# Weight conversion of a fused attention and mixer kernel: a compare-and-multiply on VectorE becomes a maximum on GpSimd

## The chip, the cores and the metric

The kernel runs on one core of one Trainium2 chip. The metric is device time in microseconds (us) of one execution, as the median of several runs. The engines are TensorE (PE in the rows, its weight loads PEld), VectorE (DVE), ScalarE (ACT), GpSimd (POOL) and SyncE (SP, which issues most DMAs). Each engine works through its own queue in order.

## The reference, cut to what matters

Three stages follow one another: attention inside clusters, a channel mixer with a gate, and a token and channel mixer. All inputs are float32. The weights of the two mixers reach the kernel as 64-bit words.

```
xr = mu_r*x + (1-mu_r)*x_prev ; xk = mu_k*x + (1-mu_k)*x_prev
k  = relu(xk @ w_k) ; v = (k*k) @ w_v ; x = sigmoid(xr @ w_r) * v
h  = relu(x^T @ w_tok1) @ w_tok2 ; u = x + h^T
out = u + relu(u @ w_ch1) @ w_ch2
```

Shapes: batch 2, sequence 768, model width 512, w_k 512x1024, w_v 1024x512, w_r 512x512, w_tok1 768x256, w_tok2 256x768, w_ch1 512x1536, w_ch2 1536x512.

## The kernel before, in words

The attention stage (up to about 200 us) is laid out by a planner and is the same in both kernels. The mixers are matrix products in which each operand is split into a high and a low part, and three products (high by high, high by low, low by high) are added in PSUM.

Weights come in units of 128 x 512 values: wr 0 to 3 (gate), wk and wv 0 to 7 (first mixer), w1 and w2 0 to 2 (token mixing), c1 and c2 0 to 11 (channel mixing), 52 conversions in all with wk 0 and wv 0 loaded a second time. A DMA brings a unit as 64-bit words into a ring of five buffers (`wraw`), seen as two interleaved 32-bit halves, `low` and `high`. `w_split` turns it into a float32 value in `g` and then into the two parts of `wu`. In the kernel before the steps are: a shift and mask of `high` (VectorE, L460), the sign bits joined in (VectorE, L464), the absolute value of `high` (ScalarE, L468, into the second half of `wu`), the bits of `low` joined in (VectorE, L470, after which the ring buffer is free and the next DMA is issued), a compare with `TINY` times the value (VectorE, L478), the rounded copy (ScalarE, L482) and the rest (VectorE, L484; GpSimd for the four wr units). The compare makes a weight zero whose `high` half, read as a float32, lies under `TINY`: the shift would have given it a wrong exponent.

`g` has two buffers, and at most two conversions are under way at once. From the end of the attention stage on (`dense[0]` is true) a list scheduler in the program, `pump`, writes out the order of the instructions: every conversion, evacuation and operand split is a `Chain`, a generator that names for each step its engine, a cost in us and whether it is a step with two SBUF inputs ("two"). `now` holds a modelled clock for each engine; `lock` keeps the modelled GpSimd steps ("G") and the two-input VectorE steps apart. The scheduler takes, of the steps that can start first, the one of the chain with the earliest due time. What it decides fixes the queue of each engine.

The first mixer runs over f = 0 to 7 for batch 0 and back for batch 1: 24 matmuls of wk f (L1354) make the hidden part f, ScalarE and VectorE square and split it (L1323 to L1329, `hl`), and 18 matmuls with wv f (L1392) add to the output, one f behind. While batch 0 runs, VectorE and ScalarE also prepare the mixed operand of batch 1 (`mk1`: L555, L557, L564, L566, four parts). The token mixer follows (L1448, L1534), then the channel mixer.

Of the kernel before, what the change touches and what calls it, by code (L numbers as in the profile page):

```python
# [13 lines left out]
AF = mybir.ActivationFunctionType  # L14
ALU = mybir.AluOpType
# [3 lines left out]
P = 128  # L19
B, H, S, D = 2, 8, 768, 64  # L20
# [19 lines left out]
TINY = 2.0**-15 * 1.125  # L40
# [258 lines left out]
def f32(ap):  # L299
    return ap.bitcast(F32)  # L300
# [3 lines left out]
def cluster_attention_moe_mixer(ctx: ExitStack, tc, q, k, v, cent, mu_k, mu_r, w_k, w_v, w_r, w1, w2, wc1, wc2, out):  # L304
    nc = tc.nc
# [38 lines left out]
            nc.gpsimd.memset(t[:, :, 0:1], 0.0)  # L344


    now = {"P": 0.0, "A": 0.0, "D": 0.0, "G": 0.0, "S": 0.0, "N": 0.0, "R": 0.0}
    lock = [0.0, 0.0]
    pipe = []

# [59 lines left out]
    dense = [False]  # L410
# [29 lines left out]
    def w_issue():  # L440
        key = seq.pop(0)
        ring.append(ring.pop(0))
        raw = ring[-1][0].tile([P, 1024], U32, tag=ring[-1][1], name="wraw")
        src = unit_src(*key)
        dst = raw.rearrange("p (k f) -> p k f", f=src.shape[-1]) if len(src.shape) == 3 else raw
        nc.sync.dma_start(out=dst, in_=src)
        now["S"] = max(now["S"], now["D"])
        staged.append((key, max(now["S"], now["D"]) + RAW_US, raw.rearrange("p (f w) -> p f w", w=2)))

    def w_split():  # L450
        key, landed, raw = staged.pop(0)
        low, high = raw[:, :, 0], raw[:, :, 1]
        pool, tag, freed = free_slots.pop(0)
        t = pool.tile([P, 2, 512], F32R, tag=tag, name="wu")

        def gen():
            yield "D", 0.45, False
            g = cvt.tile([P, 512], U32, tag="g", name="g")
            gf = f32(g)
            nc.vector.tensor_scalar(  # L460
                g, high, 3, 0x3FFFFFF8, op0=ALU.logical_shift_left, op1=ALU.bitwise_and
            )
            yield "D", 0.62, True
            nc.vector.scalar_tensor_tensor(  # L464
                out=g, in0=high, scalar=0xC0000000, in1=g, op0=ALU.bitwise_and, op1=ALU.bitwise_or
            )
            yield "A", 0.56, False
            nc.scalar.activation(t[:, 1, :], f32(high), AF.Abs)  # L468
            yield "D", 0.62, True
            nc.vector.scalar_tensor_tensor(  # L470
                out=g, in0=low, scalar=29, in1=g, op0=ALU.logical_shift_right, op1=ALU.bitwise_or
            )
            if wanted:
                spare.append((ring.pop(0), wanted.clear())[0])
            elif dense[0] and seq:
                w_issue()
            yield "D", 0.62, True
            nc.vector.scalar_tensor_tensor(  # L478
                out=gf, in0=f32(t[:, 1, :]), scalar=TINY, in1=gf, op0=ALU.is_ge, op1=ALU.mult
            )  # L480
            yield "A", 0.55, False
            nc.scalar.activation(t[:, 0, :], gf, AF.Copy)  # L482
            yield ("G", 1.4, True) if key[0] == "wr" else ("D", 0.62, True)
            (nc.gpsimd if key[0] == "wr" else nc.vector).tensor_tensor(  # L484
                out=t[:, 1, :], in0=gf, in1=f32(t[:, 0, :]), op=ALU.subtract
            )
            if key in again_from:
                yield "S", 0.55, False
                nc.sync.dma_start(out=again_from[key], in_=f32(t).rearrange("p a f -> p (a f)"))

        ch = Chain(gen(), due.get(key, 0.0), max(landed, freed))
        active[:] = [c for c in active if not c.done] + [ch]
        units[key] = (t, ch)
        slot_of[key] = (pool, tag)
        return ch
# [18 lines left out]
    def feed():  # L514
        while staged and free_slots and staged[0][0] not in units and sum(not c.done for c in active) < 2:
            w_split()
        while reloads and free_slots and not staged and not seq:
            w_reload()
        for wait in list(later):
            if wait[0]():  # L520
                later.remove(wait)
                wait[1]()
# [3 lines left out]
    def need(key):  # L526
        while key not in units:
            if not dense[0]:
                if not staged:
                    w_issue()  # L530
                w_split()
            else:
                pump(None)
        t, ch = units[key]
        after(ch)
        return t
# [82 lines left out]
    with ExitStack() as actx:  # L619
# [453 lines left out]
        def want(n, key, j=0.0):  # L1073
            return T_FIRST + PER * (n + (EARLY.get(n, LATE.get(n - NP, {})).get(key, DUE[key]) + j) / NTASK)
# [62 lines left out]
        for n in range(NP):  # L1137
# [22 lines left out]
            if n + 1 < NP:  # L1160
# [13 lines left out]
                t = o = simt_[n] = Op("P", 0.66, want(n, "simt"), act("simt"), [o], tail=0.2, need=1)  # L1174
# [37 lines left out]
        for i in range(NEARLY + 2):  # L1212
            t = want(NP - 5, f"wr{i}", NTASK * i) if i < KD else want(NP - 1, "wl", i - KD)
            landed.append(Op("S", 0.5, t - 60 if i < KD else t - 10, w_issue, [conv[i - NSTG][3]] if i >= NSTG else [], kb=512))
            if i >= NEARLY:
                continue
            back = ("G", 1.4, t, True) if i < KD else ("D", 0.62, t, True)
            conv.append(steps(w_split, [("D", 0.36, t, False), ("D", 0.62, t, True), ("A", 0.56, t, False), ("D", 0.62, t, True),
                                        ("D", 0.62, t, True), ("A", 0.55, t, False), back],
                              [landed[i]] + ([conv[i - 2][6]] if i > 1 else [])))  # L1220
        for b in range(B):
            m = Mixed(b, 1)
            mr.append(m)
            for c in range(KD - b):
                t = want(NP - 1, f"x{b}", c * DUE["xs"])
# [640 lines left out]
```

## Time and profile before

| | |
|---|---|
| median of 3 runs | 610.81 us (610.58 to 611.84) |
| profiled execution, its own time | 610.07 us |
| its span in the trace | 608.3 us |
| TensorE busy | 595.6 us |
| VectorE busy | 506.2 us |
| GpSimd busy | 123.1 us |

The span is what the trace shows between the first and the last instruction; 1.8 us of the run's own time lie around it. Times in the rows are counted from the start of the span. A busy TensorE is not the same as TensorE at its peak.

### The profile page before, as it was taken

Reading aid. Unit: us, or ns where it says so; the run is one execution under the profiler, and the core shown is the slowest. Engines: PE = TensorE matmul, PEld = TensorE weight load, DVE = VectorE, ACT = ScalarE, POOL = GpSimd, SP = SyncE. Lnnn points to the kernel's source line nnn. Section 1 sums busy time; section 2 is a strip of 40 time slices with the busy share of each in tenths; the row PEclk is TensorE's granted clock in tenths of the full one; section 3 lists DMA queues with packets and bytes.
Section 4 is the critical chain, followed back from the end, with each engine's and each line's share of the span. In section 5 each row is a group of like instructions: output and inputs, shape, how many; then the busy total and the mean of one; then the engine's idle time right before and its main releaser. Section 6 shows DMA issues by size and latency. Waiting matters only on the chain.

```text
span 608.3 us, 9503 instructions
## 1 busy us (share of the span) xinstructions
PE 595.6 (98%) x3273; PEld 489.9 (81%) x3273; DVE 506.2 (83%) x946; ACT 354.2 (58%) x667; POOL 123.1 (20%) x166
## 2 busy tenths in 40 slices
PE   7899999999999999999999999999999999999997
PEld 6667757667577668999999998888999999898895
DVE  6899899899999986999869889869959988766633
ACT  5888788889888757967756666133344323222210
POOL 4445743736622551000000000020110000000000
PEclk9999999999999999999999999999999999999999
DMA  8258859789647450434104358252564002243002
GB/s 290 77 173 250 211 149 271 177 249 271 185 135 192 142 164 22 163 127 148 50 34 129 116 183 295 74 138 76 159 148 139 35 2 109 76 132 134 2 0 105
DMA packets 40928, 84.09 MB, mean 138 GB/s; under 512 B 8816, under 2 KB 21616, under 8 KB 40880
## 3 DMA queue, kind: packets, MB, share of 16 engines
q1 hardware_dynamic: 38448, 76.01, 40.8%
q0 software_dynamic: 2432, 7.47, 5.2%
q8 instruction: 26, 0.43, 0.3%
q14 instruction: 22, 0.18, 0.1%
HBM read 51.42 MB, written 8.65 MB: 99 GB/s over the span
## 4 chain that ended last, share of the span: by engine, by line
PE 83%; DVE 7%; DMA 4%; ACT 3%; issue 2%; SPq 1%; DVEq 0%; ACTq 0%
PE ps L1354 19%; PE ps L1392 18%; PE ps L944 9%; PE ps L861 8%; PE ps L1654 8%; PE ps L1666 7%; PE ps L612 5%; PE ps L928 3%; DVE junk L869 2%; DMA t<-k_dram 2%; ACT e L878 2%; PE ps L1448 1%; PE ps L1534 1%; PE ps L691 1%; DMA kb<-mst 1%
## 5 line engine op out<-in xcount | busy, mean ns | idle before, releaser
L1392 PE MATMUL ps<-wu,hl 128*128 128x512 f32 x486 | 115.2, 391 | 0.0
L1392 PEld LDWEIGHTS ps<-wu,hl 128*128 128x128 f32 x486 | 90.8, 188 | 18.0
L878 ACT ACTIVATE e<-ps,nm 128x768 f32<-128x768 f32 x96 | 86.5, 903 | 18.6 <-DVE junk L869 16.8
L869 DVE TENSOR_SCALAR_CACHE_REDUCE junk<-ps 128x768 bf16<-128x768 f32 x96 | 90.3, 941 | 7.3 <-PE ps L861 5.2
L1354 PE MATMUL ps<-xmix,wu 128*128 128x384 f32 x384 | 69.2, 335 | 0.0
L1354 PEld LDWEIGHTS ps<-xmix,wu 128*128 128x128 f32 x384 | 67.3, 188 | 1.1
L861 PE MATMUL ps<-ka,qa 128*128 128x384 f32 x192 | 57.5, 381 | 1.1 <-ACT e L878 0.6
L482 ACT ACTIVATE wu<-g 128x512 fp32r<-128x512 f32 x52 | 32.8, 631 | 43.7 <-DVE g L478 43.6
L1654 PE MATMUL ps<-wu,hl 128*128 128x512 f32 x216 | 54.7, 393 | 0.0
L1354 PE MATMUL ps<-ut,wu 128*128 128x384 f32 x288 | 52.5, 336 | 0.5 <-DVE ut L1506 0.5
L1354 PEld LDWEIGHTS ps<-ut,wu 128*128 128x128 f32 x288 | 50.5, 188 | 1.9 <-DVE ut L1506 1.0
L861 PE MATMUL ps<-kb,qb 80*128 80x384 f32 x192 | 50.2, 343 | 1.1 <-DVE qb L805 0.7
L1493 POOL DMA_DIRECT2D uperm<-ublk x16 | 7.9, 503 | 200.9 <-ACT h L1435 164.1
L928 PE MATMUL ps<-ident,e 128*128 128x128 f32 x288 | 43.1, 277 | 3.0 <-ACT e L878 3.0
L1654 PEld LDWEIGHTS ps<-wu,hl 128*128 128x128 f32 x216 | 40.2, 188 | 6.6
L907 DVE STREAM_TRANSPOSE tb<-e 128x768 f32<-128x768 f32 x48 | 45.3, 962 | 0.0
L1713 ACT ACTIVATE hl<-t 128x384 fp32r<-128x384 f32 x24 | 12.6, 525 | 55.1 <-DVE t L1709 55.1
L861 PEld LDWEIGHTS ps<-ka,qa 128*128 128x128 f32 x192 | 30.2, 192 | 17.7 <-issue 7.8
L464 DVE SCALAR_TENSOR_TENSOR g<-wraw,g 128x512 uint32<-128x512 uint32 x52 | 41.2, 792 | 1.0
L928 PEld LDWEIGHTS ps<-ident,e 128*128 128x128 f32 x288 | 34.9, 142 | 7.3 <-ACT e L878 4.7
L1709 DVE TENSOR_TENSOR t<-ps,t 128x384 f32<-128x384 f32 x42 | 22.8, 555 | 21.1 <-PE ps L1666 20.0
L478 DVE SCALAR_TENSOR_TENSOR g<-wu,g 128x512 f32<-128x512 f32 x52 | 35.9, 689 | 3.6
(144 smaller groups left out, 1087.7 us busy)
## 6 DMA issues: line engine op xcount, KB each, us to landing
ptd<-tb SPq DMA_DIRECT2D x88, 144.0 KB, 4.6
wraw<-moe_w_ch_dram SPq DMA_DIRECT2D x24, 512.0 KB, 4.0
t<-q_dram SPq DMA_DIRECT2D x16, 384.0 KB, 4.8
t<-k_dram SPq DMA_DIRECT2D x16, 384.0 KB, 5.0
ptd<-tb POOLq DMA_DIRECT2D x40, 144.0 KB, 4.8
spill<-wu SPq DMA_DIRECT2D x10, 512.0 KB
wu<-spill SPq DMA_DIRECT2D x10, 512.0 KB, 4.4
wraw<-moe_w_k_dram SPq DMA_DIRECT2D x9, 512.0 KB, 5.2
```

The source lines that it names most:

```text
L464: nc.vector.scalar_tensor_tensor(out=g, in0=high, scalar=0xC0000000, in1=g, op0=ALU.bitwise_and, op1=ALU.bitwise_or)
L478: nc.vector.scalar_tensor_tensor(out=gf, in0=f32(t[:, 1, :]), scalar=TINY, in1=gf, op0=ALU.is_ge, op1=ALU.mult)
L861: nc.tensor.matmul(ps[:, nh, 0:HS], x[:, e, c0 : c0 + P], y[:, e, nh * HS : (nh + 1) * HS], start=first, stop=not first,)
L869: nc.vector.tensor_scalar(junk, PS_[t][:, :, 0:HS], -SCALE, None, op0=ALU.mult, op1=ALU.min, accum_out=nm)
L878: nc.scalar.activation(et.rearrange("p (a b) -> p a b", a=2), PS_.pop(t)[:, :, 0:HS], AF.Exp, bias=NM_.pop(t), scale=SCALE, accum_out=ss_[ ...
L907: nc.vector.transpose(out=T_[n][:, :, e, :, i, :].rearrange("p j k q -> p k j q"), in_=E_.pop(t).rearrange("p (k j c) -> p k j c", j=4, c=32),
L928: nc.tensor.transpose(ps[:, kk], E_[t][:, kt * P : (kt + 1) * P], ident)
L944: nc.tensor.matmul(o, vts[n][:, e, kt, :], m, start=(kt == 0), stop=(kt == NT - 1))
L1354: nc.tensor.matmul(ps[:, 0:HS], u[:, wl, c, :], xin(xl, c, sl), start=(n == 0), stop=(n == 11))
L1392: nc.tensor.matmul(accs[st], prev[:, xl, st * P : (st + 1) * P], u[:, wl, :], start=(idx == 1 and n == 0), stop=(idx == nf and n == 2),)
L1654: nc.tensor.matmul(accs[st], self.hl[q][k][:, xl, st * P : (st + 1) * P], u[:, wl, :], start=(left[st] == 2 * np_ - 1 and n == 0), stop=(l ...
L1666: nc.tensor.matmul(ps[:, 0:HS], a(wl, c), b(xl, c), start=(n == 0), stop=(n == 5))
```

## The change

The change applies to the 47 units that are split after the attention stage (`late`); the five before it (wr 0 to 3 and wk 0) keep the old steps. For the 47, the absolute value of `high` is taken first and goes into `g`, GpSimd raises it to at least `TINY` in place, and VectorE's shift and mask reads `g` instead of `high`. The compare-and-multiply is left out: a tiny weight comes out as 2^-126 with its sign instead of zero. The GpSimd step is charged to a modelled clock of its own, "K", which `lock` does not touch.

```
-    now = {"P": 0.0, "A": 0.0, "D": 0.0, "G": 0.0, "S": 0.0, "N": 0.0, "R": 0.0}
+    now = {"P": 0.0, "A": 0.0, "D": 0.0, "G": 0.0, "S": 0.0, "N": 0.0, "R": 0.0, "K": 0.0}
...
+        late = dense[0]
+
         def gen():
-            yield "D", 0.45, False
+            if late:
+                yield "A", 0.56, False
+            else:
+                yield "D", 0.45, False
             g = cvt.tile([P, 512], U32, tag="g", name="g")
             gf = f32(g)
+            if late:
+                nc.scalar.activation(gf, f32(high), AF.Abs)
+                yield "K", 0.8, False
+                nc.gpsimd.tensor_scalar(gf, gf, TINY, None, op0=ALU.max)
+                yield "D", 0.45, False
             nc.vector.tensor_scalar(
-                g, high, 3, 0x3FFFFFF8, op0=ALU.logical_shift_left, op1=ALU.bitwise_and
+                g, g if late else high, 3, 0x3FFFFFF8, op0=ALU.logical_shift_left, op1=ALU.bitwise_and
             )
...
-            yield "A", 0.56, False
-            nc.scalar.activation(t[:, 1, :], f32(high), AF.Abs)
+            if not late:
+                yield "A", 0.56, False
+                nc.scalar.activation(t[:, 1, :], f32(high), AF.Abs)
...
-            yield "D", 0.62, True
-            nc.vector.scalar_tensor_tensor(
-                out=gf, in0=f32(t[:, 1, :]), scalar=TINY, in1=gf, op0=ALU.is_ge, op1=ALU.mult
-            )
+            if not late:
+                yield "D", 0.62, True
+                nc.vector.scalar_tensor_tensor(
+                    out=gf, in0=f32(t[:, 1, :]), scalar=TINY, in1=gf, op0=ALU.is_ge, op1=ALU.mult
+                )
```

Lines move by 12 in most of the file. In the changed kernel the absolute value is L466, the maximum L468, the shift and mask L470, the sign L474, the low bits L481, the rounded copy L494 and the rest L496; `hl` is L1341, and the mk1 steps are L569 and L578 on VectorE.

The first place is VectorE's queue at the start of the first mixer, just after the last step of wk 1. Before, the rows end with the last step of wk 2 (`wu_2879`):

```order
L470 SCALAR_TENSOR_TENSOR g_2867<-wraw_2699,g_2867 128x512
L478 SCALAR_TENSOR_TENSOR g_2867<-wu_2861,g_2867 128x512
L460 TENSOR_SCALAR g_2904<-wraw_2701 128x512
L464 SCALAR_TENSOR_TENSOR g_2904<-wraw_2701,g_2904 128x512
L1329 TENSOR_TENSOR hl_2863<-rl_2896,hl_2863 128x384
L484 TENSOR_TENSOR wu_2861<-g_2867,wu_2861 128x512
L460 TENSOR_SCALAR g_2932<-wraw_2703 128x512
L1329 TENSOR_TENSOR hl_2863<-rl_2919,hl_2863 128x384
L470 SCALAR_TENSOR_TENSOR g_2904<-wraw_2701,g_2904 128x512
L478 SCALAR_TENSOR_TENSOR g_2904<-wu_2879,g_2904 128x512
L1329 TENSOR_TENSOR hl_2910<-rl_2938,hl_2910 128x384
L484 TENSOR_TENSOR wu_2879<-g_2904,wu_2879 128x512
```

The same place in the changed kernel, where each L470 waits for a maximum on GpSimd of the same `g`; the middle of the stretch, up to the last step of wk 2:

```order
L1341 TENSOR_TENSOR hl_2860<-rl_2885,hl_2860 128x384
L474 SCALAR_TENSOR_TENSOR g_2880<-wraw_2699,g_2880 128x512
L481 SCALAR_TENSOR_TENSOR g_2880<-wraw_2699,g_2880 128x512
L1341 TENSOR_TENSOR hl_2860<-rl_2907,hl_2860 128x384
L496 TENSOR_TENSOR wu_2873<-g_2880,wu_2873 128x512
L470 TENSOR_SCALAR g_2901<-g_2901 128x512
L474 SCALAR_TENSOR_TENSOR g_2901<-wraw_2701,g_2901 128x512
L481 SCALAR_TENSOR_TENSOR g_2901<-wraw_2701,g_2901 128x512
L1341 TENSOR_TENSOR hl_2903<-rl_2937,hl_2903 128x384
L470 TENSOR_SCALAR g_2929<-g_2929 128x512
L474 SCALAR_TENSOR_TENSOR g_2929<-wraw_2703,g_2929 128x512
L496 TENSOR_TENSOR wu_2879<-g_2901,wu_2879 128x512
```

The compare (L478) has gone from the queue, and a conversion that had its first two steps done ahead of wk 1 (`g_2867`, wv 1) now has all of them behind it (one L470 of `g_2880` stands just ahead of these rows).

The second place is VectorE's queue before the last step of wk 5 (`wu_3118` before, `wu_3133` in the changed kernel). Before:

```order
L478 SCALAR_TENSOR_TENSOR g_3100<-wu_3078,g_3100 128x512
L464 SCALAR_TENSOR_TENSOR g_3123<-wraw_2979,g_3123 128x512
L484 TENSOR_TENSOR wu_3078<-g_3100,wu_3078 128x512
L470 SCALAR_TENSOR_TENSOR g_3123<-wraw_2979,g_3123 128x512
L478 SCALAR_TENSOR_TENSOR g_3123<-wu_3118,g_3123 128x512
L460 TENSOR_SCALAR g_3171<-wraw_3012 128x512
L464 SCALAR_TENSOR_TENSOR g_3171<-wraw_3012,g_3171 128x512
L484 TENSOR_TENSOR wu_3118<-g_3123,wu_3118 128x512
```

And in the changed kernel:

```order
L496 TENSOR_TENSOR wu_3078<-g_3087,wu_3078 128x512
L569 SCALAR_TENSOR_TENSOR t_3080<-xT1_98,mu_90,t_3079 128x768
L470 TENSOR_SCALAR g_3147<-g_3147 128x512
L474 SCALAR_TENSOR_TENSOR g_3147<-wraw_2985,g_3147 128x512
L481 SCALAR_TENSOR_TENSOR g_3147<-wraw_2985,g_3147 128x512
L470 TENSOR_SCALAR g_3155<-g_3155 128x512
L474 SCALAR_TENSOR_TENSOR g_3155<-wraw_3031,g_3155 128x512
L481 SCALAR_TENSOR_TENSOR g_3155<-wraw_3031,g_3155 128x512
L1341 TENSOR_TENSOR hl_3163<-rl_3185,hl_3163 128x384
L496 TENSOR_TENSOR wu_3133<-g_3147,wu_3133 128x512
```

A step of mk1 (L569) and three steps of the unit after it (`g_3155`) now stand ahead of wk 5's last step. From the last step of wk 1 to that of wk 5 the queue held 8 rows each of L460, L464, L470, L478, L484 and L1329 before. In the changed kernel it holds 9 each of L470, L474, L481 and L1341, 8 of L496, 3 of L569 and 1 of L578; the mk1 steps used to come after wk 5. Seven of the nine L474 are followed at once by the L481 that reads their result.

The third place is GpSimd's queue from the gate's operands (L578) to the end. Before, only the 16 DMA issues for `uperm` stood behind the L566 rows. In the changed kernel:

```order
L578 TENSOR_TENSOR xmix<-t,xmix 128x768 x5
L468 TENSOR_SCALAR g<-g 128x512 x31
L1505 DMA uperm<-ublk 32x768 x8
L468 TENSOR_SCALAR g<-g 128x512 x7
L1505 DMA uperm<-ublk 32x768 x7
L468 TENSOR_SCALAR g<-g 128x512
L1505 DMA uperm<-ublk 32x768
L468 TENSOR_SCALAR g<-g 128x512 x8
```

The 47 maxima share that queue with the DMA issues, in three blocks.

## Rows read from the trace of the kernel before

**Rows 1.** The page: span, and busy time by engine (share, count).

```profile
span 608.3 us, 9503 instructions
PE 595.6 (98%) x3273; PEld 489.9 (81%) x3273; DVE 506.2 (83%) x946; ACT 354.2 (58%) x667; POOL 123.1 (20%) x166
```

**Rows 2.** TensorE's waits from 240 us on: total us, times, longest us.

```profile
PEld ps L1354 <- DVE ut L1506: 1.0, 2, 0.8
PEld ps L1666 <- DVE t L1709: 0.4, 1, 0.4
```

**Rows 3.** Busy us by engine in two stretches, then clock, DMA share, GB/s.

```profile
core 0: us, PE busy (x) PEld busy (x) DVE busy (x) ACT busy (x) POOL busy (x), PEclk, DMA share, GB/s
240.00:260.00 20.00, 20.00 (x106) 18.59 (x105) 18.95 (x32) 17.79 (x33) 0.00 (x0) 1.00 0.40 132
280.00:300.00 20.00, 20.00 (x103) 18.28 (x103) 18.99 (x30) 14.30 (x24) 0.00 (x0) 1.00 0.36 106
```

**Rows 4.** Timeline of TensorE: start us, us, line, operation, tiles, count.

```profile
256.27 4.35 PE L1354 MATMUL ps<-xmix,wu 128*128 128x384 f32 x24
...
281.19 4.35 PE L1354 MATMUL ps<-xmix,wu 128*128 128x384 f32 x24
...
489.11 1.23 PE L1354 MATMUL ps<-ut,wu 128*128 128x384 f32 x6
```

**Rows 5.** Groups by line: count, then busy us, mean ns, idle before.

```profile
L478 DVE SCALAR_TENSOR_TENSOR g<-wu,g 128x512 f32<-128x512 f32 x52 | 35.9, 689 | 3.6
...
L637 POOL CAST kb<-t 64x768 fp32r<-64x768 f32 x16 | 13.5, 855 | 40.4 <-PE ps L861 29.3 <-DMA t<-k_dram 10.8
...
L484 POOL TENSOR_TENSOR wu<-g,wu 128x512 fp32r<-128x512 f32 x4 | 5.2, 1295 | 0.3
L884 POOL TENSOR_SCALAR ss<-ss 128x6 f32<-128x6 f32 x16 | 4.2, 262 | 35.4 <-ACT e L878 35.0
```

**Rows 6.** Timelines of VectorE and GpSimd where both work, 208 to 214 us.

```profile
208.71 4.53 DVE L464 SCALAR_TENSOR_TENSOR g<-wraw,g 128x512 uint32<-128x512 uint32 x1
...
209.03 3.65 POOL L566 TENSOR_TENSOR xmix<-t,xmix 128x768 fp32r<-128x768 f32 x2
212.77 0.56 POOL L884 TENSOR_SCALAR ss<-ss 128x6 f32<-128x6 f32 x1
```

**Rows 7.** Timeline of VectorE in the first mixer, batch 0, and one later row.

```profile
245.43 0.69 DVE L464 SCALAR_TENSOR_TENSOR g<-wraw,g 128x512 uint32<-128x512 uint32 x1
246.04 0.68 DVE L484 TENSOR_TENSOR wu<-g,wu 128x512 fp32r<-128x512 f32 x1
246.65 0.68 DVE L470 SCALAR_TENSOR_TENSOR g<-wraw,g 128x512 uint32<-128x512 uint32 x1
247.43 0.69 DVE L478 SCALAR_TENSOR_TENSOR g<-wu,g 128x512 f32<-128x512 f32 x1
248.04 0.42 DVE L460 TENSOR_SCALAR g<-wraw 128x512 uint32<-128x512 uint32 x1
248.50 0.69 DVE L464 SCALAR_TENSOR_TENSOR g<-wraw,g 128x512 uint32<-128x512 uint32 x1
249.24 0.56 DVE L1329 TENSOR_TENSOR hl<-rl,hl 128x384 fp32r<-128x384 f32 x1
249.71 0.68 DVE L484 TENSOR_TENSOR wu<-g,wu 128x512 fp32r<-128x512 f32 x1
...
276.33 0.68 DVE L484 TENSOR_TENSOR wu<-g,wu 128x512 fp32r<-128x512 f32 x1
...
296.84 0.96 DVE L566 TENSOR_TENSOR xmix<-t,xmix 128x768 fp32r<-128x768 f32 x1
297.72 1.01 DVE L557 SCALAR_TENSOR_TENSOR t<-xT,mu,t 128x768 f32<-128x768 f32 x1
298.65 0.42 DVE L460 TENSOR_SCALAR g<-wraw 128x512 uint32<-128x512 uint32 x1
...
480.76 0.69 DVE L484 TENSOR_TENSOR wu<-g,wu 128x512 fp32r<-128x512 f32 x1
```

## The prediction

> **What bounds the kernel now.** I read the page first: TensorE is busy for 595.6 of a span of 608.3 us, VectorE for 506.2 [rows 1]. Then TensorE's waits over the mixers, where the change acts: 1.0 us for the operand of the channel mixer and 0.4 us for a sum in its second half, nothing else [rows 2]. So TensorE runs through from 240 us almost to the end, and work taken from another engine can give back 1.4 us at most. What the reader is to see next is how little room VectorE has behind it: in the two stretches of the first mixer it is busy for 18.95 and 18.99 of 20 us, while GpSimd does nothing [rows 3]. VectorE's timeline against TensorE's shows how far ahead the weights are: the last step of wk 5 ends at 276.33 + 0.68 = 277.01 us, and TensorE starts on wk 5 at 281.19 [rows 4, 7], a margin of 4.2 us. Later the margins are wider: c1 10 ends at 481.45 and is needed at 489.11 [rows 4, 7]. The question is therefore not what VectorE saves, but whether the first mixer's weights still come in time.
>
> **What goes.** 47 L478 of 0.689 us [rows 5], 32.4 us of VectorE's time. In the queue one takes 0.61 us (247.43 to 248.04) [rows 7]. None of it is on TensorE's path, so by itself it is worth nothing but margin.
>
> **What comes.** 47 maxima of 128 x 512 on GpSimd. The trace has none of that size, so I bound it by GpSimd's own rows. A scalar operation on 6 elements takes 0.262 us and a one-input conversion of 768 elements 0.855 us [rows 5]: 0.778 ns per element, so 512 elements take 0.262 + 506 x 0.778 = 0.66 us. From below stands 0.262 us, from above the two-input operation of the same size, 1.295 us [rows 5]. I take 0.66, because the maximum has one input. The absolute value changes place, not price. The shift and mask reads a packed `g` instead of every second word; I leave it at its 0.46 us in the queue (248.04 to 248.50) [rows 7].
>
> **The two engines don't add up.** At 208.71 us a VectorE step with two SBUF inputs took 4.53 us; a like one at 245.43 took 0.69. In between GpSimd ran 3.65 us, from 209.03 on [rows 6, 7]. The difference, 3.8 us, is GpSimd's time: VectorE stood until GpSimd had finished. It holds the other way, for a GpSimd step with one input: the one at 212.77, which met the end of that VectorE step, took 0.56 us where the mean is 0.262 [rows 5, 6]. The Trainium skill says the same in "SBUF — State Buffer", section "Who interferes with whom": VectorE and GpSimd share a pair of ports under an exclusive lock. The trace agrees, with the 4.53 us. Almost every VectorE step of the first mixer has two SBUF inputs, so I charge each maximum to VectorE in full: 0.66 us comes where 0.61 us goes. VectorE has won nothing.
>
> **The planner thinks it has.** The maximum is charged to a clock of its own, outside the lock, so the planner sees 0.62 us less VectorE work in each unit and moves other work forward. This is the queue from the last step of wk 1 (246.04 + 0.68 = 246.72 us) to that of wk 5, by start-to-start times in VectorE's timeline [rows 7]: L460 0.46, L464 0.61, L470 0.78 (the next row needs its result), L478 0.61, L484 0.61, L1329 0.47, L557 0.93, L566 0.88.
> Before, eight conversions and eight L1329: 8 x 3.07 + 8 x 0.47 = 28.3 us. It took 277.01 - 246.72 = 30.3, so 2.0 us were waits.
> After: 9 L470 x 0.46 = 4.14; 7 L474 with the reader right behind x 0.78 and 2 x 0.61 = 6.68; 9 L481 x 0.61 = 5.49; 8 L496 x 0.61 = 4.88; 9 L1341 x 0.47 = 4.23; 3 L569 x 0.93 and 1 L578 x 0.88 = 3.67. Together 29.1 us, and 9 maxima x 0.66 = 5.9, in all 35.0 us.
> So wk 5 ends at 246.7 + 35.0 = 281.7 us without any wait, 0.5 us after TensorE needs it, and 2.5 us after with the 2.0 us of waits that the same stretch had. Two things pull apart here. GpSimd can take its turn in a wait of VectorE's, which speaks for the low end. But there are new waits: the absolute value now writes `g` and stands in ScalarE's queue until VectorE's last step on the old `g`; behind it wait ScalarE's relu and square, which release TensorE's PSUM; the maximum waits for the absolute value, and L470 for the maximum, with every evacuation behind it in VectorE's queue. That speaks for the high end, and I take 2.0 us.
> The same list gives wk 2 (13 rows, three maxima, 9.4 us) at 256.1 us against a need at 256.27 [rows 4]: no stall without waits, some tenths with them. These lates don't add: once TensorE has waited, all later needs move with it.
>
> **What costs nothing.** wk 1: its steps of the new kind run while VectorE and ScalarE wait for each other over the gate's operands. The 16 DMA issues for `uperm` behind maxima in GpSimd's queue: the maximum ahead of the first eight belongs to a unit that is split before the sums which these DMAs move; the last of the second eight stands behind one more maximum, about 1 us, for an operand that TensorE reads only in the channel mixer's second half. Late units of the channel mixer lose some tenths each at the worst out of 7.7 us. If that cover went, each would cost TensorE its own lateness.
>
> **The sum.** 0 from the attention stage, +2.0 in the first mixer, 0 from the two waits of [rows 2], which hang on TensorE's own results and a DMA. The profiled execution took 610.07 us (608.3 of span [rows 1] and 1.8 around it), so 612.1 for it; the median of the runs, 610.81, lies 0.7 above it, so 612.8 us for the median.
> The Trainium skill's "GPSIMD Engine Reference", section 3.1, measures 769 ns for a tight loop over 512 elements. By it the nine maxima take 1.0 us more, and my estimate would be 613.8 us; no run here shows it.
>
> **The rivals.**
> *No stall.* GpSimd's maxima slip into VectorE's waits, or don't hold it up. Without them wk 5 ends at 246.7 + 29.1 + 2.0 = 277.8 us, 3.4 us in time, and the time stays at 610.8. For it: one-input steps on GpSimd that hold up VectorE are not in the trace, only the reverse. It decides at 3.4 / 9 = 0.38 us charged per maximum. 27%.
> *A dearer maximum.* At 1.295 us the nine cost 5.7 us more, and so does TensorE's wait: 618.5 us. For it: GpSimd's price for a maximum is unknown. Against: one input. 10%.
> *Faster.* VectorE, freer in the channel mixer, brings the operand and the sum of [rows 2] in time: 1.4 us, 609.4. It needs both waits gone, and the chain ahead of the first is TensorE, a transposition and a DMA, in which no compare stands. 5%.
> *My forecast*, a stall of 0.5 to 4 us: 58%.
>
> **How the numbers follow.** About 0.2%, 1.2 us, is what a measurement can tell from no change. The forecast's low end lies inside it, some 6 of its 58%. So slower has 52 + 10 = 62%, the same 27 + 6 = 33%, faster 5%. For the range I leave out the faster case and the outer half of the dear one: from 610.6, just under no stall, to 616.0, a stall of 5.2 us or 1.0 us per maximum.
>
> **What would show it.** In the changed profile: TensorE idle for 1 to 3 us between 255 and 300 us, before L1366 (the old L1354), ended by VectorE's L496; maxima of 0.6 to 0.8 us; VectorE steps of 1.2 us and more beside a maximum, where 0.69 was the rule; the mk1 steps earlier than before. If L474 and L481 keep 0.69 us while GpSimd works, the lock is not there for this operation, and the no-stall rival holds. If TensorE waits for something other than a weight unit, such as a PSUM bank behind ScalarE, the step on the queue is wrong though the sign may hold.

## The result, and the profile after

The changed kernel takes 618.29 us (median of 6 runs, 616.79 to 620.93), the kernel before beside it 610.69 (6 runs, 610.0 to 612.24): a ratio of 1.0134, 95% interval 1.011 to 1.0158. It is slower by 7.6 us, where 2.0 were forecast.

The page of the changed kernel, with span, busy times and the group of the maximum; it answers to [rows 1]:

```profile
span 616.5 us, 9527 instructions
...
PE 600.2 (97%) x3273; PEld 489.7 (79%) x3273; DVE 485.2 (79%) x899; ACT 354.6 (58%) x667; POOL 199.6 (32%) x213
...
L468 POOL TENSOR_SCALAR g<-g 128x512 f32<-128x512 f32 x47 | 77.5, 1654 | 147.4 <-ACT g L466 120.4
```

VectorE is busy for 21 us less than before, GpSimd for 77 us more, and one maximum takes 1.65 us, not 0.66.

Where the time went is read best from the line of TensorE's first products, which opens the mixers (with `xmix`) and runs into the channel mixer (with `ut`). The instructions of a line, their count, shortest, median and longest time, and first and last start; first of the kernel before, then of the changed one:

```profile
L1354 PE MATMUL ps<-xmix,wu x384: 333/334/346, 243.8 to 368.2; 128*128 128x384 f32 x192
L1354 PE MATMUL ps<-ut,wu x288: 333/334/446, 409.2 to 501.4; 128*128 128x384 f32 x144
```

```profile
L1366 PE MATMUL ps<-xmix,wu x384: 332/334/443, 244.5 to 370.1; 128*128 128x384 f32 x192
L1366 PE MATMUL ps<-ut,wu x288: 331/334/446, 414.7 to 509.7; 128*128 128x384 f32 x144
```

From the first start to the last it is 501.4 - 243.8 = 257.6 us before and 509.7 - 244.5 = 265.2 after: 7.6 us. I call this the length of the mixers; it leaves out the stages ahead of them, whose end moved between 242.0 and 245.8 us over all profiles of this study, also between kernels with the same order of instructions (242.4 to 245.0), and what follows the last start, which took the same time in both (608.3 - 501.4 = 106.9 and 616.5 - 509.7 = 106.8 us). The median matmul has not changed (334 ns). TensorE's busy time in the page is 4.6 us longer with the same 3273 matmuls, so a part of its waits seems to be counted there as busy, and I go by the length instead. TensorE waits, and its waits are these (changed kernel, from 225 us on; us in total, times, longest), in the place of [rows 2]:

```profile
PEld ps L1366 <- DVE hl L1347: 2.9, 4, 1.4
PEld ps L1546 <- DVE h L1449: 2.6, 2, 1.7
PEld ps L1366 <- DVE ut L1518: 1.3, 3, 0.6
PEld ps L1366 <- DVE wu L496: 1.0, 3, 0.5
PEld ps L1546 <- ACT h L1447: 0.8, 1, 0.8
PEld ps L1366 <- ACT wu L494: 0.5, 1, 0.5
```

The weights (`wu`) cost 1.5 us. The larger waits are for evacuations: the hidden part of the channel mixer (`hl`, L1347) and that of the token mixer (`h`, L1447 and L1449), neither of which the change touches. What holds them up stands in VectorE's waits:

```profile
DVE g L470 <- POOL g L468: 19.4, 20, 1.6
```

VectorE stands 19.4 us at the head of its queue, at the shift and mask, for a maximum. One of these in the channel mixer, in the timelines of the three engines (start, us; in brackets the idle time before and what ended it):

```profile
462.80 1.63 POOL L468 TENSOR_SCALAR g<-g 128x512 f32<-128x512 f32 x1 [2.58 <-ACT g L466]
...
464.46 0.43 DVE L470 TENSOR_SCALAR g<-g 128x512 uint32<-128x512 uint32 x1 [1.38 <-POOL g L468]
464.81 0.69 DVE L496 TENSOR_TENSOR wu<-g,wu 128x512 fp32r<-128x512 f32 x1
465.41 0.55 DVE L1347 SCALAR_TENSOR_TENSOR hl<-ps,hl 128x384 fp32r<-128x384 f32 x1
...
466.01 1.16 PE L1366 MATMUL ps<-ut,wu 128*128 128x384 f32 x5 [1.12 <-DVE hl L1347]
```

The maximum ends at 464.43 us. VectorE has waited 1.38 us for it and goes on at 464.46; the evacuation, two places behind in the queue, ends at 465.96, and TensorE starts at 466.01 after 1.12 us without work. The token mixer shows it over a longer stretch, again the three engines:

```profile
377.23 2.94 POOL L468 TENSOR_SCALAR g<-g 128x512 f32<-128x512 f32 x2 [5.68 <-ACT g L466]
...
378.75 0.82 DVE L470 TENSOR_SCALAR g<-g 128x512 uint32<-128x512 uint32 x1 [1.44 <-POOL g L468]
379.62 0.69 DVE L474 SCALAR_TENSOR_TENSOR g<-wraw,g 128x512 uint32<-128x512 uint32 x1
...
383.40 3.67 DVE L1429 TENSOR_TENSOR x<-ps,sg 128x512 f32<-128x512 f32 x6
...
388.19 0.68 DVE L1449 SCALAR_TENSOR_TENSOR h<-ps,h 128x512 fp32r<-128x512 f32 x1
...
391.80 0.68 DVE L1449 SCALAR_TENSOR_TENSOR h<-ps,h 128x512 fp32r<-128x512 f32 x1
...
388.93 2.34 PE L1546 MATMUL ps<-h,wu 128*128 128x512 f32 x9 [0.52 <-DVE h L1449]
392.54 0.72 PE L1546 MATMUL ps<-h,wu 128*128 128x512 f32 x2 [1.27 <-DVE h L1449]
```

Two conversions that wait for their maxima put the evacuations of the first mixer (L1429) behind them, these the two L1449, and TensorE stands 0.52 and 1.27 us for them. The same rows speak against the lock as the prediction had it: the second maximum runs until 380.17, and L474 at 379.62 lies four fifths inside it and takes 0.69 us, as ever. Only L470, the one-input step, is longer there, 0.82 for 0.42.

The windows that answer to [rows 3], changed kernel:

```profile
core 0: us, PE busy (x) PEld busy (x) DVE busy (x) ACT busy (x) POOL busy (x), PEclk, DMA share, GB/s
240.00:260.00 20.00, 19.60 (x99) 17.47 (x98) 17.23 (x27) 17.09 (x31) 6.87 (x5) 1.00 0.32 105
280.00:300.00 20.00, 20.00 (x100) 17.77 (x99) 19.23 (x30) 14.20 (x28) 7.76 (x4) 1.00 0.41 133
```

The granted clock is 1.00 in both. TensorE loses 0.4 us near wk 2, where [rows 4] had no gap, and shows no idle time near wk 5. There the timelines have these rows; by the order of the queue the first is the last step of wk 5, and the second, cut off by the end of the window, is TensorE's start on wk 5:

```profile
282.45 0.68 DVE L496 TENSOR_TENSOR wu<-g,wu 128x512 fp32r<-128x512 f32 x1
...
282.98 3.25 PE L1366 MATMUL ps<-xmix,wu 128*128 128x384 f32 x17
```

### The profile page after: what moved, and what is told of

It reads as the page before. It is cut to its first block, busy times and chain, and to the rows that moved or that the text cites. A ratio compares the mean times of both kernels' runs of the same rounds, so it can differ in the third digit from the quotient of the medians.

```text
span 616.5 us, 9527 instructions
## 1 busy us (share of the span) xinstructions
PE 600.2 (97%) x3273; PEld 489.7 (79%) x3273; DVE 485.2 (79%) x899; ACT 354.6 (58%) x667; POOL 199.6 (32%) x213
## 4 chain that ended last, share of the span: by engine, by line
PE 60%; DVE 16%; ACT 11%; POOL 5%; DMA 4%; issue 4%; SPq 1%; DVEq 0%; ACTq 0%; POOLq 0%
PE ps L1404 9%; PE ps L873 8%; PE ps L1366 8%; PE ps L956 8%; PE ps L1666 8%; PE ps L1678 7%; POOL g L468 5%; PE ps L940 4%; PE ps L624 3%; DMA kb<-mst 2%; DVE g L474 2%; DVE wu L496 2%; ACT g L466 2%; DVE g L470 2%; DVE junk L881 2%
## 5 line engine op out<-in xcount | busy, mean ns | idle before, releaser
L468 POOL TENSOR_SCALAR g<-g 128x512 f32<-128x512 f32 x47 | 77.5, 1654 | 147.4 <-ACT g L466 120.4
L494 ACT ACTIVATE wu<-g 128x512 fp32r<-128x512 f32 x52 | 32.7, 628 | 53.7 <-DVE g L481 52.6
L466 ACT ACTIVATE g<-wraw 128x512 f32<-128x512 f32 x47 | 31.2, 670 | 23.0 <-DVE wu L496 23.0
L474 DVE SCALAR_TENSOR_TENSOR g<-wraw,g 128x512 uint32<-128x512 uint32 x52 | 40.5, 779 | 1.0
```

Source lines behind the costliest of these rows:

```text
L466: nc.scalar.activation(gf, f32(high), AF.Abs)
L468: nc.gpsimd.tensor_scalar(gf, gf, TINY, None, op0=ALU.max)
L474: nc.vector.scalar_tensor_tensor(out=g, in0=high, scalar=0xC0000000, in1=g, op0=ALU.bitwise_and, op1=ALU.bitwise_or)
```

## The experiments

Theory 1: VectorE waits at the head of its queue for a maximum that lasts longer than the order of the queues was made for, and evacuations and weights behind it come late. Theory 2, near to the prediction: contention, GpSimd's work lengthens VectorE's steps. Theory 3: the order alone, made new because the compare left VectorE's list. All kernels below are edits of the changed one; ratios are against the kernel before on the same chip, with their 95% intervals, and "mixers" is the length defined above against 257.6 us.

**The maximum on 8 columns.**

```
-nc.gpsimd.tensor_scalar(gf, gf, TINY, None, op0=ALU.max)
+nc.gpsimd.tensor_scalar(gf[:, 0:8], gf[:, 0:8], TINY, None, op0=ALU.max)
```

> The maximum is taken on 8 of 512 columns, so the other weights are not raised; every queue is the same row for row. One maximum should take about 0.27 us. Theory 1 (VectorE waits for a long maximum): all stalls beyond those of the kernel before go, 610.5 to 611.7 us. Theory 2 (contention): the same, as nothing is left to contend, 610.5 to 611.7. Theory 3 (the new order by itself): the order is unchanged, so 616 to 618.5 us.

610.26 us, ratio 1.0007 (0.9989 to 1.0025); mixers 500.8 - 243.3 = 257.5:

```profile
L1366 PE MATMUL ps<-xmix,wu x384: 333/334/346, 243.3 to 367.7; 128*128 128x384 f32 x192
L1366 PE MATMUL ps<-ut,wu x288: 333/334/446, 408.7 to 500.8; 128*128 128x384 f32 x144
```

All of the loss is gone with the order unchanged, so theory 3 falls for this order. The time lies a little under the range of theories 1 and 2, as the next one lies under that of theory 1; the kernel before took 609.88 us on that chip, where the ranges were reckoned from 610.69. It also shows what the change could win at best: VectorE is rid of 32 us of work and nothing is faster.

**On 160 columns**, the price that the prediction assumed, **and on 320.** The edits are as above with 160 and 320.

> The maximum is taken on 160 of 512 columns, so the other weights are not raised; the order is unchanged. By the measured 1.487 us for 512 columns and 0.262 us for 6, one should take 0.64 us: the price that the prediction assumed, and under the 0.8 that the scheduler assumes. Theory 1: nearly no stall, 610.7 to 612 us. The prediction's own account (at this price VectorE is delayed through the lock, and a weight unit of the first mixer comes 2 us late): 612.8 us with TensorE waiting for wu. Theory 3 (order alone): 616 to 618.5 us.

609.53 us, ratio 0.999 (0.9968 to 1.0012); mixers 500.9 - 243.3 = 257.6.

> The maximum on 320 of 512 columns (the other weights are not raised), order unchanged: by the rows about 1.02 us, 0.2 over the scheduler's 0.8. With 0.66 there was no loss and with 1.65 one of 8 us. If the loss begins where the maximum outlasts what the scheduler allows: 610.5 to 613.5 us. If it grows from zero in proportion to the time: nearly half, 613.5 to 615 us.

610.8 us, ratio 1.002 (1.0005 to 1.0035); mixers 257.9. The maxima in these kernels and in the changed one (count, shortest, median and longest ns, first and last start), with 160, 320 and 512 columns:

```profile
L468 POOL TENSOR_SCALAR g<-g x47: 596/663/1272, 236.0 to 473.6; 128x160 f32<-128x160 f32 x47
```

```profile
L468 POOL TENSOR_SCALAR g<-g x47: 997/1067/1672, 235.9 to 475.0; 128x320 f32<-128x320 f32 x47
```

```profile
L468 POOL TENSOR_SCALAR g<-g x47: 1486/1619/2229, 237.3 to 484.2; 128x512 f32<-128x512 f32 x47
```

At 0.66 us, the price of the prediction, there is no stall beyond the waits of before: its "no stall" rival would have held. The loss isn't in proportion either: 0.0, 0.3 and 7.6 us in the mixers at 0.66, 1.07 and 1.62 us. VectorE's waits for the maxima are 6.9 us in the first of these kernels, 12.1 in the second and 19.4 in the third; the 12.1 us cost TensorE 0.3, so nearly all of them fell into time that VectorE had to spare.

**Contention without waiting.** The maximum on 8 columns and behind it one of 384 columns on a dead tile, which nobody waits for.

```
+nc.gpsimd.tensor_scalar(gf[:, 0:8], gf[:, 0:8], TINY, None, op0=ALU.max)
+scr = f32(ohs.rearrange("p h i a b -> p (h i a b)"))
+nc.gpsimd.tensor_scalar(scr, scr, TINY, None, op0=ALU.max)
```

> The maximum on g is cut to 8 of 512 columns (the other weights are not raised), and right behind it GpSimd takes a maximum of 384 columns on a tile that nobody reads any more; every other queue is row for row that of the changed kernel. By the rows so far that is 0.30 + 1.18 us of GpSimd's work in a unit, about the 1.49 of the changed kernel, but VectorE waits for the first 0.30 alone, or for a scratch maximum only where two units follow closely. Theory 1 (waiting): the stalls mostly stay away, 610 to 612.5 us. Theory 2 (contention): nearly the changed kernel's loss, 615 to 618 us.

611.83 us, ratio 1.0017 (0.9991 to 1.0042); mixers 503.1 - 245.0 = 258.1. The groups of GpSimd and the timelines of both engines in a stretch of the first mixer:

```profile
L468 POOL TENSOR_SCALAR oh<-oh 128x384 f32<-128x384 f32 x47 | 66.5, 1414 | 0.0
L468 POOL TENSOR_SCALAR g<-g 128x8 f32<-128x8 f32 x47 | 20.7, 440 | 130.6 <-ACT g L466 103.1 <-DVE hl L1341 27.6
```

```profile
349.36 1.69 POOL L468 TENSOR_SCALAR oh<-oh 128x384 f32<-128x384 f32 x1
...
349.33 0.69 DVE L481 SCALAR_TENSOR_TENSOR g<-wraw,g 128x512 uint32<-128x512 uint32 x1
349.94 0.72 DVE L470 TENSOR_SCALAR g<-g 128x512 uint32<-128x512 uint32 x1
350.78 0.69 DVE L496 TENSOR_TENSOR wu<-g,wu 128x512 fp32r<-128x512 f32 x1
```

GpSimd has more to do than in the changed kernel (66.5 + 20.7 = 87.2 against 77.5 us). Of the steps beside its maximum only L470 is longer, 0.72 for 0.42; the maximum itself stretches, 1.69 us where it takes 1.16 at best. The busy times of this kernel, and below them those with 8 columns and no scratch maximum:

```profile
PE 597.1 (98%) x3273; PEld 489.8 (80%) x3273; DVE 485.5 (80%) x899; ACT 355.7 (58%) x667; POOL 207.0 (34%) x260
PE 595.4 (98%) x3273; PEld 490.1 (81%) x3273; DVE 475.9 (78%) x899; ACT 356.3 (59%) x667; POOL 142.7 (23%) x213
```

VectorE's steps are 9.6 us longer in all, 0.2 us for each scratch maximum and as much as in the changed kernel (485.2 busy). So its contention is all there, and TensorE loses at most half a microsecond by it. Theory 2 falls.

**Waiting with little data.** Six maxima of 8 columns, one after the other on the same columns.

```
+for _ in range(6): nc.gpsimd.tensor_scalar(gf[:, 0:8], gf[:, 0:8], TINY, None, op0=ALU.max)
```

> In place of one maximum of 512 columns six of 8 columns, one after the other on the same columns (the other weights are not raised): some 1.4 to 1.8 us that VectorE must wait for, with 48 columns of data in place of 512 to contend over. The order is unchanged. Theory 1 (waiting): the changed kernel's loss, 615.5 to 619 us, with VectorE's waits for GpSimd near 19 us. Theory 2 (contention): 610 to 611.5 us.

627.51 us, ratio 1.0276 (1.023 to 1.0321); mixers 518.3 - 242.4 = 275.9, 18.3 more. The six took 99.0 / 47 = 2.11 us, more than I had reckoned. VectorE's waits here:

```profile
DVE g L470 <- POOL g L468: 36.7, 28, 2.0
```

So 48 columns of data cost more than 512 do: theory 1, beyond its own range. VectorE's two-input steps keep 0.69 us in it, and its L470 takes 0.43, so VectorE waits and is not slowed. Not all of the 18.3 us is VectorE's waiting, though. After two of TensorE's stalls its granted clock lies at 0.50, the lower of its two levels (1.2 and 2.4 GHz), for 3.4 us each (columns as in [rows 3]):

```profile
258.00:261.40 3.40, 3.40 (x12) 3.40 (x12) 2.21 (x5) 2.64 (x5) 2.82 (x8) 0.51 0.45 154
462.90:466.30 3.40, 3.40 (x11) 3.40 (x12) 3.33 (x7) 1.31 (x3) 0.64 (x2) 0.50 0.00 0
```

The 23 matmuls from 257.00 us and the 12 from 462.82 take 5.85 and 3.92 us, where as many in the same places of the changed kernel take 4.26 and 2.36: some 3.2 us of the loss. In no other profile of this study did the clock fall in the mixers. One of TensorE's stalls has another root, in the same kernel's timelines:

```profile
449.09 1.82 POOL L468 TENSOR_SCALAR g<-g 128x8 f32<-128x8 f32 x6
450.85 0.61 POOL L1505 DMA_DIRECT2D uperm<-ublk  x1
...
460.04 1.76 ACT L1516 ACTIVATE ut<-uperm 128x384 fp32r<-128x384 f32 x4 [6.98 <-DMA wraw<-moe_w_ch_dram]
...
462.82 2.59 PE L1366 MATMUL ps<-ut,wu 128*128 128x384 f32 x7 [5.15 <-DVE hl L1347]
```

The last `uperm` DMA goes out behind maxima, ScalarE stands 7 us at its first read of `uperm` with an evacuation behind it, and TensorE loses 5.15 us. The profile names another DMA as the releaser; that the late one is meant I infer from the operand, and the times agree: the longest `uperm` transfer of this kernel landed 9.2 us after its issue, and 450.85 + 9.2 is 460.05. Without this stall and the lower clock about 10 us of the 18.3 are left, an estimate by subtraction.

**The scheduler told the price.**

```
-yield "K", 0.8, False
+yield "K", 1.7, False
```

> Only the scheduler's cost of the maximum changes, from 0.8 to 1.7 us; the instructions are those of the changed kernel in another order. Theory 1 (VectorE stands at the head of its queue for a maximum that takes longer than the scheduler believes): the shift and mask is now placed after the maximum's real end, VectorE's waits for GpSimd fall from some 20 us to a few, and the time to 611 to 613 us. Theory 2 (contention: GpSimd's work itself lengthens VectorE's steps until weights and evacuations are late): as much GpSimd work as before, so 617 to 619 us. Theory 3 (the order changed because the compare left VectorE's list, whatever the maximum costs): 615 to 619 us.

615.9 us, ratio 1.0101 (1.0056 to 1.0146); mixers 509.1 - 245.6 = 263.5. VectorE's waits for the maximum fall to 11.9 us and not to a few, and 5.9 us of the loss stay, now at `ut` (3.9 us, 1.0 before), `wu` (1.9) and `hl` (1.8). Theory 1 in its first form, that the scheduler's error is the cause, was wrong here. The time lies in the range of theory 3; this order was not run with a short maximum, so what the order alone costs here is not shown.

**The price told, six short maxima.** The two edits together.

> As the six narrow maxima in place of one (the other weights are not raised), but with the scheduler's cost of the step at 1.7 us, so in the order that took 615.9 us with full maxima. Theory 1, with the order to blame for what was left there: 615 to 617 us. Theory 2, in which what was left there is contention that no order removes: 610 to 612 us.

624.52 us, ratio 1.0228 (1.0187 to 1.0269); mixers 514.8 - 243.8 = 271.0. Neither range: waiting of 105.8 / 47 = 2.25 us a unit was not ordered away by the price either, while its contention is next to none (two-input steps of VectorE at 0.69 us).

**Three conversions under way, and two as a control.** In both the scheduler knows the price, the absolute value and the maximum work in two buffers of their own, and one of the five ring buffers is given up for the space; they differ in one number.

```
+a = pre[0].tile([P, 512], U32, tag="a", name="a")
+nc.scalar.activation(f32(a), f32(high), AF.Abs)
+yield "K", 1.7, False
+nc.gpsimd.tensor_scalar(f32(a), f32(a), TINY, None, op0=ALU.max)
...
-sum(not c.done for c in active) < 2
+sum(not c.done for c in active) < 3
```

> The scheduler knows the price (1.7 us), the absolute value and the maximum work in two buffers of their own, so that the buffers of g are held only from the shift and mask on, and up to three conversions may be under way; one ring buffer of five is given up for the space. If what was left with the price known (615.9 us) came from too few conversions under way, so that a longer one comes late whatever the order: 610.5 to 612.5 us. If it came from the order alone or from contention: 615 us or more.

> The control for three conversions: the same buffers and the same price, but two conversions under way. By either theory near the kernel with only the price changed, 614 to 617 us; if it is as fast as with three, the buffers or the ring did it and not the number under way.

Three: 612.93 us, ratio 1.0072 (1.0046 to 1.0098). Two: 616.15 us, ratio 1.0127 (1.0092 to 1.0163). The products' line with three:

```profile
L1382 PE MATMUL ps<-xmix,wu x384: 333/334/440, 245.8 to 370.4; 128*128 128x384 f32 x192
L1382 PE MATMUL ps<-ut,wu x288: 333/334/443, 411.4 to 504.2; 128*128 128x384 f32 x144
```

And with two:

```profile
L1382 PE MATMUL ps<-xmix,wu x384: 331/334/442, 243.3 to 369.2; 128*128 128x384 f32 x192
L1382 PE MATMUL ps<-ut,wu x288: 333/334/446, 411.0 to 507.5; 128*128 128x384 f32 x144
```

With three the mixers take 504.2 - 245.8 = 258.4 us, 0.8 more than before; with two it is 507.5 - 243.3 = 264.2, 6.6 more. The buffers by themselves win nothing (6.6 against the 5.9 of the price alone). VectorE's waits for a maximum are 2.3 us with three and 10.2 with two. So in the profiled execution maxima of 1.77 us on average are nearly hidden when three conversions overlap; with two conversions none of the three orders run with a full maximum hid them. The order of the queues follows from the number, so the two are not told apart.

The medians say less. Three lies in neither of its ranges, 3.0 us above the kernel before, of which its mixers explain 0.8; two lies 6.3 above. In the profiled execution with three the mixers begin 2.0 us later than in that of before (245.8 against 243.8), and the granted clock from 25 to 50 us, in the attention stage, was 0.86 there against 0.93: that part is not the conversions' doing. But four of its five executions had a mean clock of 0.994, and their median of 613.5 us is 2.5 above that of the five executions of the kernel before at 0.993 or 0.994 on that chip (610.98). So the clock does not explain all of the difference, and what does is not shown.

**The first mixer alone.** 512 columns for wk and wv, 8 for the rest.

```
+c = 512 if key[0] in ("wk", "wv") else 8
+nc.gpsimd.tensor_scalar(gf[:, 0:c], gf[:, 0:c], TINY, None, op0=ALU.max)
```

> The full maximum for the 17 units of the first mixer only; 8 columns for the other 30 (not raised otherwise); the order is unchanged. The trace of the changed kernel has about 1.0 us of TensorE's stalls in the first mixer, 2.7 in the token mixer and 3 in the channel mixer. If stalls add up by place (theories 1 and 2 both): 1 us above the kernel with 8 columns everywhere, 610.8 to 612.5 us. If the prediction's place were right and the rest a consequence of lateness carried along: 615 us or more.

611.46 us, ratio 1.0015 (0.9995 to 1.0036); mixers 503.0 - 244.3 = 258.7:

```profile
L1366 PE MATMUL ps<-xmix,wu x384: 332/334/446, 244.3 to 369.9; 128*128 128x384 f32 x192
L1366 PE MATMUL ps<-ut,wu x288: 333/334/446, 410.9 to 503.0; 128*128 128x384 f32 x144
```

The first mixer's maxima cost 1.1 us, so by difference the other 6.5 us hang on the 30 maxima behind it.

**On VectorE, or shared.**

```
-nc.gpsimd.tensor_scalar(gf, gf, TINY, None, op0=ALU.max)
+nc.vector.tensor_scalar(gf, gf, TINY, None, op0=ALU.max)
```

> The maximum moves from GpSimd to VectorE, where the scheduler charges it 0.45 us; GpSimd does nothing in the mixers but issue DMAs. One should take about 0.42 us there, like the shift and mask. VectorE then has 0.42 + 0.42 in a unit where before it had 0.42 + 0.69. Theories 1 and 2 (the loss comes through GpSimd, by waiting or by contention): 610.3 to 612 us. Theory 3 (the compare's leaving and the absolute value's moving to the front upset the order): 613 us or more.

612.32 us, ratio 1.0037 (1.0016 to 1.0057); mixers 500.8 - 242.0 = 258.8. That is between the two ranges. One takes 0.42 us. The scheduler has made a new order here, in which TensorE waits 1.5 us for `wu` early in the first mixer; so theory 3 may hold for this order.

```
+nc.gpsimd.tensor_scalar(gf[:, 0:160], gf[:, 0:160], TINY, None, op0=ALU.max)
+yield "D", 0.8, False; nc.vector.tensor_scalar(gf[:, 160:512], gf[:, 160:512], TINY, None, op0=ALU.max)
```

> The whole maximum, but GpSimd takes 160 columns and VectorE the other 352, which should cost VectorE some 0.3 us in a unit, charged as 0.35. VectorE's work is then 0.3 + 0.42 where before it was 0.42 + 0.69, and GpSimd's stays at the harmless 0.66 us. Theory 1: 609.5 to 611.5 us, the kernel before at best, since no more than 1.4 us of waits is left to win. If the order alone decides which stalls appear: anything up to 613.

611.23 us, ratio 1.003 (1.0011 to 1.0049); mixers 504.5 - 244.8 = 259.7. Both keep the whole maximum, and their mixers lose 1.2 and 2.1 us, under a third of what the change loses. Neither beats the kernel before: TensorE had 1.4 us of waits in it, and none of these removes them.

## Why the prediction was wrong

**What bounds the kernel** was right: TensorE runs through the mixers, VectorE's savings are worth nothing by themselves, and the time is lost as waits of TensorE.

**"I take 0.66, because the maximum has one input"** is the first step that failed. It measured 1.62 us as the median and 1.49 undisturbed. The value was taken from a conversion of 768 elements (0.855 us in [rows 5]), and the upper bound from the two-input operation, 1.295 us; the maximum lies above both.

**"I charge each maximum to VectorE in full"** failed by itself: the second maximum on a dead tile, 1.41 us on average, lengthened VectorE's steps by 0.2 us a unit, less than the 0.38 at which the prediction itself lets "no stall" win. What [rows 6] show for two-input steps on both engines does not carry over to this operation, and the rule of the Trainium skill ("SBUF — State Buffer", section "Who interferes with whom"), that VectorE and GpSimd share a pair of ports under an exclusive lock, does not either, as I applied it: L474 kept 0.69 us inside a maximum. Contention exists (L470 0.82 for 0.42; a few L474 and L481 near 1.1 and 1.0), but it comes to 0.5 us of TensorE's time. The prediction's own sign for that, steps of 0.69 us beside a maximum, was to speak for no stall; it came, and the stall came by another way.

**"L470 waits for the maximum, with every evacuation behind it in VectorE's queue"** was in the prediction, as a reason for the high end of one stall. It was the mechanism of nearly the whole loss.

**The place.** Of the two stalls spoken of, the small one near wk 2 came (0.4 us in the window), the large one at wk 5 did not. VectorE's queue was late there about as reckoned, its last step of wk 5 ending at 283.13 us against a forecast of 281.7 to 283.7, but that is luck: VectorE's work was not lengthened by 0.66 us a maximum, and 2.3 us of the stretch were waits at L470. TensorE's need had moved with the earlier waits and the later start of the mixers, and it began wk 5 at 282.98 without a gap. It could begin before 283.13 because the first of its products reads only the rounded copy of the unit, so the margin counted up to the start was a little too strict. The first mixer gave 1.1 us of 2.0.

**"What costs nothing"** is the step that cost most. It asked only whether weights come late, and the units of the token and channel mixer had margins of microseconds. But a conversion with wide margin still stands in VectorE's queue ahead of evacuations with none, and the prediction itself had named those. From there came 6.5 of the 7.6 us, by the run with full maxima in the first mixer only. The `uperm` DMAs cost little in the changed kernel (`ut` 1.3 us of waits, 1.0 before), and 5 us where the maxima were longer still.

**The rivals.** The "dearer maximum" rival gave 618.5 us, within 0.2 of the measured median. Its price was nearest, but its place (nine maxima of the first mixer, through the lock) was not, so the agreement is chance.

What stays open: the loss that remains with the price known and two conversions under way goes with their number in the profiles, while by the medians about half of it stays with three; which wait of which unit starts it, and what the order alone adds to it, is not shown.

## What to carry to other kernels

When a step leaves a busy engine for an idle one, price the handoff, not the work: how long does the next instruction on the busy engine stand at the head of its queue, and what without margin is queued behind it? Then ask how many such chains may overlap; here 0.66 us was free, 1.07 nearly free and 1.62 cost 7.6 us in the mixers; with a third conversion under way they lost 0.8. The price of an operation that no row shows should keep its whole range up to the end, with the case that each end makes.

## What the runs showed of the hardware

- A one-input maximum on GpSimd, 32-bit values: 0.23, 0.60, 1.00 and 1.49 us at best for 8, 160, 320 and 512 columns. That is (1.486 - 0.232) / 504 = 2.49 ns per column and 0.21 us for the start; VectorE takes 0.42 us for 512.
- In contention it was more GpSimd's instruction that stretched (384 columns: 1.16 to 1.69 us) and VectorE's one-input step (0.42 to 0.72 or 0.82), while two-input steps of VectorE mostly kept their time.
- The attention stage ended anywhere in a range of 3.8 us, seen at the start of the mixers, and the granted clock goes with it. Its mean from 25 to 50 us was 1.00 in two profiles (mixers from 242.0 and 242.4 us), 0.93 in eight (243.2 to 245.0) and 0.86 in four (244.3 to 245.8). In the kernel before it stood at 0.50 for some 3.4 us from 28.5 us on, after TensorE had waited 1.88 us up to 26.66; in the profile with the maximum on VectorE the same wait was followed by no fall. Lengths of a stage told the kernels apart where whole times hardly did.
- In the mixers the clock fell only in the kernel with six short maxima: after waits of TensorE of 0.53 and 0.94 us close together, and after one of 5.15 us. In the changed kernel, with idle times of up to 1.27 us, it stayed at 1.00.
